# The first FFN product of three blocks by seven block products, with 40 listed V-moving heads

## The chip, the cores and the metric

One core of a Trainium2 chip runs the whole program. The core has a matmul engine (TensorE, in the profile PE, its weight loads PEld), a vector engine (VectorE, DVE), an activation engine (ScalarE, ACT), a third elementwise engine (GpSimd, POOL) and an engine whose queue issues most DMAs (SyncE, SP). The metric is the device time of one execution in microseconds (us), as a median of several runs. A difference of 0.2% is about what can be told from no difference here.

## What is computed

```python
xn = layernorm(x)                                   # x: 2048 x 512
q  = xn @ wq                                        # 32 heads of 128
p  = softmax(q @ k_cache^T / sqrt(128))             # 2048 cached keys a head
s  = concat_heads(p @ v_cache) @ wo                 # wo: 4096 x 512
h  = relu(xn @ w1 + b1) ** 2                        # w1: 512 x 1792
out = x + s * silu(h @ w2 + b2)                     # w2: 1792 x 512
```

Inputs and output are bf16. Attention and the feed-forward network (FFN) read the same normalized rows; the FFN's output gates the attention's.

## The kernel before

**Tiling.** The 2,048 query rows are four blocks j = 0 to 3 of 512 rows. A block runs the 32 heads in turn; head number g = 32 j + h goes from 0 to 127. A head's 2,048 keys are eight pairs of 128-key tiles, so the kernel has 1,024 *steps* (`NPAIR`), one for each pair. At a step `pi`, `gen_scores` (L903) issues two score matmuls of 512 columns into one half of `psA`, and one ACT exponential of 1,024 columns from there into one of 8 buffers `pT` (`NPT`). `gen_pv` (L1248) issues the product with V for the pair two steps earlier.

**Two kinds of heads.** In a *V-stationary* head (called b in the code, `gen_pv_b` L962) V is the weight and the exponentials move: 16 matmuls of 512 columns, with the result transposed in one bank of `psO`. ACT copies it to `o_col`. The softmax denominators then have to be summed apart: a pT buffer goes either to DVE alone (`den_part`, 1,024 columns) or through POOL, which adds its halves into `h_sum` (`part_add`), with a DVE reduction behind it (`part_half`). The sums travel through DRAM scratch (`d_scr`, `d_quad`, `r_scr`, `r_all`: four small DMAs) and POOL multiplies `o_col` by the reciprocals into `oT`. In a *V-moving* head (a) the exponentials are the weights and V with a column of ones moves: 64 matmuls of 129 columns, with the denominator in the 129th. DVE copies both `psO` banks to `o_un` (L1292), POOL scales, and one DMA transposes `o_bf` into `oT`. `at_a` (L499) chooses the kind while the order is being written: the first two and last three heads are V-moving, and others where the planner finds enough owed DVE work.

**The rest of TensorE's work** goes in between as *jobs* that use the two banks of `psF`: query projections, the FFN's first product (`job_h` L1434: 14 chunks of 128 hidden units, each four matmuls of 512 columns), its second (`job_o2` L1461) and the output projection (`job_wo` L1507). Jobs stand in a list with a due step and a release step (L1593-L1612); `fill_one` (L1620) takes matmuls from them at an even rate.

**The seven-product form.** In blocks 1 to 3 the query projection of two heads is done together (`job_pair` L1370): the 2x2 block product of weights (two heads by two halves of the 512 inputs) and rows (two halves of 256) takes seven block products instead of eight. Each block product is two matmuls of 256 columns, so 14 in all for a pair. For it, weights are scaled by a power of two from the heads' largest entry (`chunk_start` L829: DVE maxima, two trips through DRAM), ACT scales both heads (`wp_mul`), POOL makes four sums in f16 (`wp_sums`), and the whole goes to DRAM scratch `wq_scr` (`wp_store`), to be loaded a pair at a time (`fill_pair` L871). One staging area `wq_new` serves all 16 pairs, started every 22 steps from step 80. Sums of the rows are made by POOL once a block (`x_sums`). The results come out of `psF` through `u_t` by DVE copies and additions; `scaled` (L1364) gives a copy to ACT if ACT is planned to be free within `ACT_ROOM`.

**What sets the order.** The program writes each engine's queue beforehand. A planner (`_Sched` L111, costs in `_cost` and `_ISSUE`) keeps an estimated time for each engine and for each result, and `fill_dve`, `fill_pool`, `fill_sync` and `fill_act` (L1182-L1239) choose by these which waiting piece of side work is put into a queue next, within limits such as `ROOM`, `ACT_SPARE` and `SLACK`. On the chip the queues then run in the order written, each instruction waiting for its semaphores.

W1 is kept whole in `w1_sb`; its seven loads are issued between steps 0 and 48. `job_h` is evicted by two DVE instructions of 512 columns from `psF`: bias and relu into `r_t`, then (x + bias) times `r_t` into `h2T`.

## Time and profile before

| | us |
|---|---|
| median of 3 runs | 1216.28 (1214.98 to 1216.38) |
| the profiled execution | 1217.89 |
| its span, first to last instruction | 1216.0 |
| busy: TensorE / DVE / ACT / POOL | 1201.2 / 1074.1 / 1095.4 / 1044.5 |
| ACT: 1,024 columns of exponentials, one | 1.025 |
| DMA: mean busy share of the 16 engines, main queue | 84.8% |
| TensorE's granted clock | 1.000 |

| instruction (engine) | count | mean ns |
|---|---|---|
| h_sum from pT, 512 columns (POOL) | 636 | 1158 |
| d_part from h_sum, 512 columns (DVE) | 636 | 682 |
| d_part from pT, 1,024 columns (DVE) | 212 | 1212 |
| u_t from psF, 256 columns (DVE) | 144 | 457 |
| qt_sb from psF and u_t, 256 columns (DVE) | 144 | 453 |
| r_t from psF, 512 columns (DVE) | 56 | 726 |
| h2T from psF and r_t, 512 columns (DVE) | 56 | 746 |
| o_un from psO, 258 columns (DVE) | 44 | 420 |
| o_col from psO, 512 columns (ACT) | 106 | 595 |
| oT from o_col and r_all (POOL) | 106 | 1281 |
| weight scaling, 512 columns (ACT) | 32 | 718 |
| weight sums, 256 columns (POOL) | 64 | 670 |

The span is what one profiled execution took between its first and last instruction. An instruction is named by output and inputs, `psA<-qt_sb,kT` for a score matmul; L235 and L240 are the helpers that issue matmuls, so groups are told apart by their tiles. A busy share near 100% for TensorE is no sign of peak speed by itself, since the ends of matmuls overlap.

### The profile page before, as it was taken

The page shows a single profiled execution, that of the slowest core. Times are in us where ns is not written, and L with a number is a line of the kernel's source. Part 1 is how long each engine was busy: PE and PEld are TensorE (multiplying, and loading weights), DVE is VectorE, ACT ScalarE, POOL GpSimd, SP SyncE. Part 2 cuts the span into 40 slices and gives each one's busy share as a digit, 9 for nine tenths or more (in the row PEclk, how much of TensorE's full clock was granted, in tenths as well). Part 3 has the DMA queues.
Part 4 walks back from the last instruction along what each step waited for, and adds up shares of the span by engine and source line. Part 5 has one row for each costly group of instructions (what it writes and reads, how often), then busy time and mean ns, then how long its engine had stood idle before and what let it go on. Part 6 is the DMA issues. An engine that isn't in the chain of part 4 may idle for free.

```text
span 1216.0 us, 21110 instructions
## 1 busy us (share of the span) xinstructions
PE 1201.2 (99%) x6952; PEld 711.7 (59%) x7085; DVE 1074.1 (88%) x2019; ACT 1095.4 (90%) x1183; POOL 1044.5 (86%) x1008
## 2 busy tenths in 40 slices
PE   9999999999999999999999999999999999999999
PEld 7555555556666565665665555666556565655566
DVE  5999999998988979879899999877998989899973
ACT  7998999999999999999989989999998989899894
POOL 2889999999888979789879989877998989799973
PEclk9999999999999999999999999999999999999999
DMA  9799999889899989897888879887797987978871
GB/s 215 176 196 220 210 215 199 224 190 217 211 222 245 210 194 226 212 199 177 198 181 193 195 185 205 180 192 170 172 215 170 192 205 163 209 159 192 193 170 45
DMA packets 509020, 235.48 MB, mean 194 GB/s; under 512 B 399184, under 2 KB 485968, under 8 KB 508912
## 3 DMA queue, kind: packets, MB, share of 16 engines
q1 hardware_dynamic: 506816, 230.06, 84.8%
q0 software_dynamic: 1424, 3.81, 1.0%
q8 instruction: 56, 0.92, 0.3%
q14 instruction: 52, 0.43, 0.1%
q10 hardware_dynamic: 672, 0.26, 0.1%
HBM read 151.52 MB, written 11.46 MB: 134 GB/s over the span
## 4 chain that ended last, share of the span: by engine, by line
PE 94%; DVE 2%; DMA 2%; issue 1%; POOL 1%; SPq 0%; ACT 0%; ACTq 0%; DVEq 0%; POOLq 0%
PE psA L235 35%; PE psO L235 29%; PE psF L235 18%; PE psO L240 6%; PE psF L240 6%; DVE d_part L303 1%; DMA wq_sb<-in_A_wq_dram 1%; POOL h_sum L248 1%; DMA kT<-in_A_k_cache_dram 0%; SPq L311 0%; DMA wq_sb<-wq_scr 0%; PE psA L240 0%; ACT pT L244 0%; DVE qt_sb L258 0%; POOL acc L248 0%
## 5 line engine op out<-in xcount | busy, mean ns | idle before, releaser
L244 ACT ACTIVATE pT<-psA 128x1024 bf16<-128x1024 f32 x1025 | 1029.5, 1025 | 99.4 <-PE psA L235 69.4
L248 POOL TENSOR_TENSOR h_sum<-pT 128x512 f32<-128x512 bf16 x636 | 720.5, 1158 | 75.9 <-ACT pT L244 53.4
L235 PE MATMUL psA<-qt_sb,kT 128*128 128x512 bf16 x1963 | 591.6, 380 | 5.2 <-ACT pT L244 1.6
L235 PE MATMUL psO<-pT,v_sb 128*128 128x512 bf16 x1659 | 496.4, 379 | 2.6 <-DVE o_un L262 0.3
L303 DVE TRANSPOSE_TENSOR_REDUCE d_part<-h_sum 128x16 f32<-128x512 f32 x636 | 423.0, 682 | 12.8 <-POOL h_sum L248 12.3
L235 PEld LDWEIGHTS psA<-qt_sb,kT 128*128 128x128 bf16 x2032 | 277.2, 145 | 167.1 <-ACT pT L244 15.3
L303 DVE TRANSPOSE_TENSOR_REDUCE d_part<-pT 128x32 f32<-128x1024 bf16 x212 | 256.1, 1212 | 3.8 <-ACT pT L244 3.1
L235 PEld LDWEIGHTS psO<-pT,v_sb 128*128 128x128 bf16 x1696 | 165.6, 98 | 148.5 <-issue 2.3
L248 POOL TENSOR_TENSOR oT<-o_col,r_all 128x512 bf16<-128x512 f32 x106 | 135.7, 1281 | 32.4 <-DMA r_all<-r_scr 32.1
L235 PE MATMUL psF<-wo_all,oT 128*128 128x512 bf16 x468 | 154.7, 379 | 0.7
L240 PEld LDWEIGHTS psO<-v_sb,pT 128*128 128x128 bf16 x1408 | 93.9, 98 | 34.9 <-issue 0.4
L240 PE MATMUL psO<-v_sb,pT 128*128 128x129 bf16 x1408 | 108.2, 220 | 0.1
L235 PE MATMUL psF<-xnT,w_sb 128*128 128x512 bf16 x220 | 73.4, 379 | 0.2
L235 PE MATMUL psF<-w_sb,h2T 128*128 128x512 bf16 x215 | 70.9, 379 | 0.4
L253 DVE TENSOR_SCALAR u_t<-psF,sc_q 128x256 f32<-128x256 f32 x144 | 65.8, 457 | 5.8 <-PE psF L240 4.6
L235 PEld LDWEIGHTS psF<-wo_all,oT 128*128 128x128 bf16 x480 | 46.8, 98 | 40.6 <-DVE qt_sb L253 0.3
L240 PE MATMUL psF<-xs_t,wq_sb 128*128 128x256 f16 x384 | 69.7, 273 | 0.1
L258 DVE SCALAR_TENSOR_TENSOR qt_sb<-psF,sc_q,u_t 128x256 bf16<-128x256 f32 x144 | 65.2, 453 | 4.8 <-PE psF L240 3.6
L244 ACT ACTIVATE o_col<-psO 128x512 f32<-128x512 f32 x106 | 63.0, 595 | 0.0
L262 DVE COPY o_un<-psO 128x258 f32<-128x258 f32 x44 | 16.7, 420 | 50.1 <-PE psO L240 50.1
L240 PEld LDWEIGHTS psF<-xs_t,wq_sb 128*128 128x128 f16 (+1 forms) x384 | 36.8, 98 | 30.2 <-DVE u_t L253 3.6
L240 PE MATMUL psF<-xnT,wq_sb 128*128 128x256 bf16 x288 | 53.8, 273 | 0.4 <-DMA wq_sb<-wq_scr 0.4
(86 smaller groups left out, 753.6 us busy)
## 6 DMA issues: line engine op xcount, KB each, us to landing
v_sb<-in_A_v_cache_dram SPq DMA_DIRECT2D x508, 128.0 KB, 3.0
r_all<-r_scr SPq DMA_DIRECT2D x106, 256.0 KB, 4.0
wq_sb<-wq_scr SPq DMA_DIRECT2D x48, 448.0 KB, 4.3
wo_all<-in_A_wo_dram SPq DMA_DIRECT2D x64, 256.0 KB, 3.5
wq_scr<-wq_sb SPq DMA_DIRECT2D x16, 448.0 KB, 3.4
wq_sb<-in_A_wq_dram SPq DMA_DIRECT2D x16, 256.0 KB, 3.7
kT<-in_A_k_cache_dram SPq DMA_TRANSPOSE x254, 3.9
wq_sb<-in_A_wq_dram SPq DMA_DIRECT2D x31, 128.0 KB, 3.5
```

The costliest lines, as they stand in the source:

```text
L235: return e.matmul(out, lhsT, rhs, start=start, stop=stop)
L240: return e.matmul(out, lhsT, rhs, start=start, stop=stop, skip_group_check=True)
L244: return e.activation(out, in_, func, bias=bias, scale=scale)
L248: return e.tensor_tensor(out, in0, in1, op)
L253: return e.tensor_scalar(out, in0, scalar1=scalar1, scalar2=None, op0=op0)
L258: return e.scalar_tensor_tensor(out=out, in0=in0, scalar=scalar, in1=in1, op0=op0, op1=op1)
L262: return e.tensor_copy(out, in_)
L303: return e.tensor_reduce(out, in_, axis=AX.X, op=ALU.add, apply_transpose=True)
```

## The change

1. **FFN1 by pairs.** Block 0 keeps `job_h`. In blocks 1-3 a new `job_h2` computes two chunks of 128 hidden units by the seven-product form of `job_pair`. Its results are kept in fp32 in a new `hb_t` (bias added in the copies out of `psF`), and a DVE instruction `relu_sq` squares them into `h2T`. W1's columns are scaled by powers of two like the query weights: seven more pairs pass the staging, with maxima (`chunk_max`) over W1's chunks and over b1; b1 is scaled with them, and W2's rows are multiplied once by the inverse squares (`w2_mul`, ACT) after block 0's second product.
2. **W1 streamed.** `w1_sb` goes. W1 passes through two slots in the memory of `xs_t` during block 0; the scaled pairs are loaded one at a time into `w1_pair` (`fill_fpair`) in blocks 1-3.
3. **Staging.** Four staging areas instead of one, two of them borrowed until steps 190 and 215; 23 pairs, one every 13 steps from step 72.
4. **pT** has 10 buffers instead of 8. `r_t` shares memory with `hb_t`.
5. **o_col** is copied by DVE instead of ACT where the planner finds ACT later than DVE (plus `COL_ACT`).
6. **V-moving heads** are a written list of 40, ten in each block.
7. **Planner constants** and the planned issue time of `r_all` change. Every job has a list of what it waits for; `fill_one` takes a job only if all of it is planned ready by now (`SOON` = 0, was 100 ns), and `fill_act` may take any ready piece, W2's last.

```diff
-          "d_quad": (530, 4200), "r_scr": (530, 2200), "r_all": (1230, 4400)}
+          "d_quad": (530, 4200), "r_scr": (530, 2200), "r_all": (530, 4400)}
...
-    ROOM = 1500
+    ROOM = 1000
     LATE = 150
-    LATE_EVICT = 250
+    COL_ACT = -400
+    COL_DVE = 0
+    LATE_EVICT = 150
     POOL_ROOM = 300
-    SLACK = 1500
-    FIRST_B = 2
-    A_OWED = (14500, 12500, 12500, 14500)
-    LATE_U = 700
-    ACT_ROOM = 500
-    ACT_SPARE = 400
+    SLACK = 1000
+    A_SET = (0, 1, 8, 10, 12, 15, 17, 20, 26, 29, 33, 36, 38, 40, 42, 44, 46, 52, 60, 62, 66, 69, 71, 73, 75, 77, 81, 84, 90, 93, 97, 99, 102, 105, 107, 110, 119, 125, 126, 127)
+    LATE_U = 200
+    ACT_ROOM = 100
+    ACT_SPARE = 300
     PAIR_BANK = (0, 1, 0, 1, 0, 0, 1)
-    A_APART = 3
     NPP = H // 2
     NRW = 2 * HC
-    WQ_PACE = 22
-    WQ_FIRST = 80
+    WQ_PACE = 13
+    WQ_UNTIL = (9999, 190, 215, 9999)
+    SOON = 0
+    NO_ACT = (0,)
+    WQ_FIRST = 72
...
-    NSL, NSW, NQS, NPT, NOT, NOC, NHS = 3, 4, 5, 8, 21, 5, 3
+    NSL, NSW, NQS, NPT, NOT, NOC, NHS = 3, 4, 5, 10, 21, 5, 3
...
-    w1_sb = sb("w1_sb", [P, NDC, F], BF16)
...
+    w1_new = xs_t[:].rearrange("p i c q -> p (i c q)").bitcast(BF16).rearrange(
+        "p (s c e) -> p s c e", s=2, c=NDC)
+    w1_pair = sb("w1_pair", [P, PW], BF16)
+    wq_new2 = sb("wq_new2", [P, PW], BF16)
+    NFP = NFC // 2
+    hb_t = sb("hb_t", [P, 2, QB], F32)
...
-    r_t = sb("r_t", [P, 2, QB], BF16)
+    r_t = hb_t[:, 0, :].bitcast(BF16).rearrange("p (s q) -> p s q", s=2)
...
+        return g in A_SET
...
+    def chunk_max(c):
+        i, x = divmod(c, 2)
+        t_fm[c] = E(DV, partial(_abs_max, out=mx_f[:, c:c + 1],
+                                in_=w1_new[:, i % 2, :, x * P:(x + 1) * P]),
+                    deps=[tok_w1[i], t_max1])
...
+    def w2_mul(c):
+        t_w2s[c] = E(AC, partial(_act, out=w2_sb[:, c, :], in_=w2_sb[:, c, :], func=ACT.Copy,
+                                 scale=sc_2[:, c:c + 1]),
+                     deps=[t_o2[0, qt] for qt in range(TPB)] + [t_sc2[0], tok_w2])
+
+    def fill_fpair(j, i):
+        t_wf[j, i] = S.emit_dma(SP, partial(_dma, out=w1_pair[:], in_=wq_scr[NPP + i]), sl_wf,
+                                deps=[t_ws[NPP + i], t_fdone.get(fprev(j, i)), t_ws.get(wp_last.get(2))])
...
+            if max(AC.t - PE.t - COL_ACT, 0) > max(DV.t - PE.t - COL_DVE, 0):
+                t_free[b] = t_col[m] = E(
+                    DV, partial(_copy, out=o_col[:, m % NOC, :], in_=bankO(b)),
+                    deps=deps, late=LATE_EVICT)
+            else:
+                t_free[b] = t_col[m] = E(
+                    AC, partial(_act, out=o_col[:, m % NOC, :], in_=bankO(b), func=ACT.Copy),
+                    deps=deps)
...
+            for fn in sorted(act_quiet, key=lambda x: x.func is w2_mul):
+                t = ready_at(fn)
+                if t is not None and t <= max(AC.t, PE.t):
+                    act_quiet.remove(fn)
+                    fn()
+                    break
...
+    def relu_sq(j, c):
+        t_h2[j, c] = E(DV, partial(_stt, out=h2T[:, c, :], in0=hb_t[:, c % 2, :], scalar=0.0,
+                                   in1=hb_t[:, c % 2, :], op0=ALU.max, op1=ALU.mult),
+                       deps=[t_hc[j, c], t_hd[j, c]] + [t_o2[j - 1, qt] for qt in range(TPB)])
+
+    def biased(out, in_, c, deps):
+        if max(AC.t, S.ready(deps)) <= PE.t + ACT_ROOM:
+            return E(AC, partial(_act, out=out, in_=in_, func=ACT.Identity, bias=b1s[:, c:c + 1]),
+                     deps=deps)
+        return E(DV, partial(_ts, out=out, in0=in_, scalar1=b1s[:, c:c + 1], scalar2=None,
+                             op0=ALU.add), deps=deps, late=LATE_U)
+
+    def job_h2(j, i):
+        c = 2 * i
+        steps = pair_steps(w1_pair, j)
+
+        def mm(n, bank):
+            y, lhs, rhs, start = steps[n]
+            b = bank ^ y
+            place, place2 = bankF(b)[:, 0:HB], bankF(bank ^ 1)[:, 0:HB]
+            for k in range(2):
+                t = E(PE, partial(_mm_shared, out=place, lhsT=lhs[:, k, :], rhs=rhs(k),
+                                  start=start and k == 0, stop=k == 1),
+                      deps=[t_wf[j, i], t_xs[j], t_bankF[b]] + tok_xT[j], inc=k == 1)
+
+            def hb_of(x, q):
+                return hb_t[:, x, q * HB:(q + 1) * HB]
+
+            old = [t_hb[0]] if i == 0 and j == 1 else [
+                t_h2[fprev(j, i)[0], 2 * fprev(j, i)[1] + x] for x in range(2)]
+
+            def keep(x, ch):
+                t_us[x] = biased(u_t[:, x, :], place, ch, [t, t_us[x], t_b1s[0]])
+                return t_us[x]
+
+            def add(x, q, u):
+                t_us[u] = E(DV, partial(_tt, out=hb_of(x, q), in0=place2, in1=u_t[:, u, :],
+                                        op=ALU.add), deps=[t, t_us[u]] + old, late=LATE_U)
+                return t_us[u]
+
+            if n in (0, 2, 4):
+                t_bankF[b] = keep(n // 2, c + n // 4)
+            if n == 1:
+                t_bankF[b] = t_hn[0] = add(0, 0, 0)
+            if n == 4:
+                t_bankF[b ^ 1] = t_hn[1] = add(1, 1, 2)
+            if n == 5:
+                t_bankF[b] = t_x = biased(hb_of(1, 0), place, c + 1, [t, t_b1s[0]] + old)
+                t_hc[j, c + 1] = t_x
+                t_hd[j, c + 1] = t_hn[1]
+                calm(now[0] + 8, partial(relu_sq, j, c + 1))
+            if n == 6:
+                t_bankF[b] = t_hc[j, c] = add(0, 1, 1)
+                t_hd[j, c] = t_hn[0]
+                calm(now[0] + 8, partial(relu_sq, j, c))
+                t_fdone[j, i] = t_xuse[j] = t
+                n_xuse[j] += 1
+                nxt = (j, i + 1) if i + 1 < NFP else (j + 1, 0)
+                if nxt[0] < NQB:
+                    sync_quiet.append(partial(fill_fpair, *nxt))
...
-                  deps=[tok_w2, t_bankF[bank], t_h2[j, n]], inc=(n == NFC - 1))
+                  deps=[t_w2s[n] if j else tok_w2, t_bankF[bank], t_h2[j, n]], inc=(n == NFC - 1))
...
+    def h2_wait(j, i):
+        x = fprev(j, i)
+        return [t_wf.get((j, i)), t_xs.get(j), t_b1s[0]] + (
+            [t_h2.get((x[0], 2 * x[1] + y)) for y in range(2)] if x else [])
+
+    def o2_wait(j):
+        return [t_h2.get((j, c)) for c in range(NFC)] + (
+            [t_w2s.get(c) for c in range(NFC)] if j else [tok_w2])
...
-        for c in range(NFC):
+        for c in range(0, NFC, 1 if j == 0 else 2):
             k = b + (SPB * 9 // 256) * c
-            jobs.append((k, max(k - 130, 4), job_h(j, c), (None, j)))
+            job, w = (job_h(j, c), partial(h_wait, j, c)) if j == 0 else (
+                job_h2(j, c // 2), partial(h2_wait, j, c // 2))
+            jobs.append((k, max(k - 130, 4), job, None, w))
...
-        return S.ready(toks) <= PE.t + 100
+        return S.ready(toks) <= PE.t + SOON
...
+                if rel > step and not force:
                     continue
-                if rel <= step or force:
-                    cur[0] = [job, 0]
-                    cur_proj[0] = None if isinstance(p, tuple) else p
-                    jobs.pop(idx)
-                    break
+                toks = wait()
+                if None in toks or not soon(toks):
+                    continue
...
-    for i, k in enumerate([4, 10, 18, 28, 38, 48]):
-        at(k, partial(load_w1, i + 1))
+    at(4, partial(load_w1, 1))
+    for i in range(2, NFP):
+        at(30 + 18 * (i - 1) + 2, partial(sync_quiet.append, partial(load_w1, i)))
...
+    order = [0, 1, 2, 3]
+    for x in range(NFP):
+        order += [NPP + x, 4 + x]
+    order += range(4 + NFP, NPP)
+    last = {}
+    for x, p in enumerate(order):
+        k = WQ_FIRST + WQ_PACE * x
+        wp_stage[p] = [y for y in ((0, 3, 1, 2)[x % 4], x % 2 * 3) if k < WQ_UNTIL[y]][0]
+        if wp_stage[p] in last:
+            wp_prev[p] = last[wp_stage[p]]
+        last[wp_stage[p]] = p
+        at(k, partial(wp_start, p))
```

## The prediction

> **What bounds the kernel now.** I read the engines' busy times first, then the chain that ended last, then the starts in the timeline, and last the waits of the engine that the chain names.
>
> ```profile
> PE 1201.2 (99%) x6952; PEld 711.7 (59%) x7085; DVE 1074.1 (88%) x2019; ACT 1095.4 (90%) x1183; POOL 1044.5 (86%) x1008
> ...
> PE 94%; DVE 2%; DMA 2%; issue 1%; POOL 1%; SPq 0%; ACT 0%; ACTq 0%; DVEq 0%; POOLq 0%
> ```
>
> TensorE (PE) is busy for 99% and carries 94% of the chain. Matmuls overlap, so busy time does not say how much is slack. The start column does (TensorE's timeline, block 1):
>
> ```profile
> 315.15 0.62 PE L240 MATMUL psO<-v_sb,pT 128*128 128x129 bf16 x8
> 315.60 0.60 PE L235 MATMUL psA<-qt_sb,kT 128*128 128x512 bf16 x2
> 316.04 0.59 PE L235 MATMUL psF<-xnT,w_sb 128*128 128x512 bf16 x2
> 316.48 0.62 PE L240 MATMUL psO<-v_sb,pT 128*128 128x129 bf16 x8
> ...
> 322.64 0.60 PE L240 MATMUL psF<-xs_t,wq_sb 128*128 128x256 f16 x4
> 323.08 0.59 PE L235 MATMUL psO<-pT,v_sb 128*128 128x512 bf16 x2
> ```
>
> From start to start, two matmuls of 512 columns take 0.44 us, four of 256 take 0.44, eight of 129 take 0.45. Over the whole trace the start-to-start distances are 0.2158, 0.1093 and 0.0567 us for one of each. Counted by weight loads, of which none is missing: 4,792 of 512 columns (2,032 scores, 1,696 V-stationary PV, 496 output projection, 448 FFN, 120 query) make 1,034 us; 688 of 256, 75; 1,408 of 129, 80; the small ones about 12. Two more: some 2 ns on each score pair's first matmul, 2 us in all, and 2.5 us after the last matmul. That is 1,206 of 1,216. TensorE is the bound at matmul pace, and all its stalls together are some 10 us, 4 of them in the opening 15 us. The rest are small, with three larger ones. The waits and the timeline around one of them:
>
> ```profile
> PEld psA L235 <- ACT pT L244: 15.3, 49, 1.3
> ...
> PE psO L235 <- DVE o_un L262: 0.3, 1, 0.3
> ```
>
> ```profile
> 113.36 0.72 ACT L244 ACTIVATE wq_sb<-wq_sb,sc_q 128x512 bf16<-128x512 bf16 x1 [1.07 <-DMA wq_sb<-in_A_wq_dram]
> ...
> 113.99 1.00 ACT L244 ACTIVATE pT<-psA 128x1024 bf16<-128x1024 f32 x1
> ...
> 115.05 0.66 PE L235 MATMUL psA<-qt_sb,kT 128*128 128x512 bf16 x2 [0.80 <-ACT pT L244]
> ```
>
> ACT stood 1.07 us at a weight scaling whose load had not landed; the exponential behind it came late, and the scores behind that. The same happened at 218 us. Measured against the normal distance, TensorE lost 0.96 and 1.02 us there, and 0.60 at 318 us where the first pair's weights landed late.
>
> **TensorE's own work.** *FFN1 of blocks 1-3:* out go 3x14x4 = 168 matmuls of 512 columns, 168 x 0.2158 = 36.3 us. In come 21 pairs x 14 of 256 columns, 294 x 0.1093 = 32.1. Sum **-4.1**. All of it lies on the bound. *V-moving heads:* the trace has 22 (44 o_un copies), the list has 40. One costs 64 x 0.0567 = 3.63 us, a V-stationary one 16 x 0.2158 = 3.45; 18 x 0.173 = **+3.1**. Its two o_un evictions (420 ns each) hold up the next head's PV: the waits name 0.3 us in 22 heads, the start distances after such heads up to 0.9. For 18 more 0.2 to 0.9, I take **+0.4**, nearer the wait that is named, since the queue in front of these copies gets shorter.
>
> The Trainium skill, "TensorE: Matmul & The Clock Gate", section "Back-to-back issue gap", gives about 81 ns per matmul of 128 columns in a stream with weight loads, and about 131 for 512. By that an added head would cost 64 x 0.081 - 16 x 0.131 = 3.1 us, an estimate from that page, and 18 of them would lose some 56 us. The 56.7 and 215.8 ns of this trace, each with its own weight load, contradict both figures; the trace decides.
>
> **DVE.** Per V-stationary head: 6 halves at 682 and 2 whole tiles at 1212 ns (636 and 212 in 106 heads), sums, turn and reciprocal 1.06 us, together 7.6; per V-moving head 2 x 0.420 + 0.173 = 1.0. 18 heads save 118 us. FFN1 now costs 42 x (726 + 746) = 61.8 us there. After: per pair 4 biased copies (457, row of u_t), 3 additions (453, row of qt_sb from u_t) and 2 squarings of 512 fp32 from SBUF. The last has no row; the 512-column PSUM product at 746 is below, a scaling from SBUF that once took 1,786 ns beside GpSimd (xn_t: 401, median 437) is above. I take 1,000. 21 x (1.83 + 1.36 + 2.0) = 109. Column maxima: 14 x 650 ns = 9. Eviction of o_col moves here when the planner finds ACT late: 0 to 88 x 674 ns = 59. Net -118 + 47 + 9 + 0..59 = -62 to -3: DVE is at most as loaded as now, and most probably 30 us lighter.
>
> "SBUF — State Buffer", section "SBUF: two separate sides", says that a DVE instruction with two SBUF inputs and GpSimd's reads take one port pair in turn, the loser blocked for the whole instruction. The 1,786 ns above fits; by that rule each of 42 squarings could wait for a 1,158 ns h_sum, about 25 us of DVE in all if half do, an estimate, which the relief covers.
>
> **GpSimd (POOL).** A V-stationary head costs 6 x 1.158 + 1.281 = 8.2, a V-moving one 1.04 + 0.18 = 1.2; -126 us, and 28 weight sums at 670 ns add 19. It gets lighter by 107.
>
> **ACT.** Adds 14 W1 scalings and 14 W2 scalings, 28 x 718 = 20 us; 18 o_col fewer, -10.7; 0 to 88 x 595 ns go to DVE. "Either engine" for the biased copies will hardly happen: the same rule for the query pairs sent 192 of 192 to DVE, and the ACT limit in it is lowered.
>
> **SyncE and DMA.** 18 x 4 small DMAs of the denominators (about 0.43 us of issue each) go, 18 transposes (1.22) come: -31 + 22; 7 loads, 7 stores, 21 W1-pair loads (0.43) add 15. W1 streamed moves seven 256 KB loads later into block 0. Nothing here issues longer than now, and K and V are loaded two heads ahead.
>
> **Stalls.** Behind a pair's product stand TensorE's next scores and PV, so each bank wait costs directly. The query pairs lost 0.42, 0.29, 0.17, 0.17, 0.13 us in places where a u_t copy was late: 1.2 us in 48 pairs, so 21 more pairs 0.5; with the longer rule of bias and hb_t 0 to 1.5, **+0.7**. Out: with DVE lighter and ten pT buffers in place of eight these and the eight stalls of 0.09 behind ACT (1.9 together) should shrink, I take -1.5 (0 to -1.9). The three late loads (2.6): four staging places let a load run ahead, and ACT takes whichever scaling is ready; but there are 23 loads for 16 and the planner still counts on landing times. Half, -1.3 (+1.2, if two in 16 become three in 23, to -2.6). Together **-2.8**.
>
> Sum: -4.1 + 3.1 + 0.4 + 0.7 - 2.8 = -2.7 us. The profiled execution took 1,217.89 us (span 1,216.0 and 1.9 around it), so 1,215.2; the median of the runs is 1.6 below the profiled one: **1,213.6 us**. With every bound at its better end (-4.1 + 3.1 + 0.2 + 0 - 4.5) it is 1,211.0.
>
> **Rivals.** *(1) It comes out even.* Pair stalls at 1.5, evictions at 0.9, late loads not cured: -4.1 + 3.1 + 0.9 + 1.5 - 1.5 = -0.1, 1,216.2. For it: what the seven products save and the added heads cost nearly cancel by rows; against it: DVE and POOL lose 30 and 107 us of load. *(2) Slower: ACT becomes the bound between steps 72 and 358.* A step there lasts 1.17 us (32 heads of 8 steps from 17 to 309 us and to 608), an exponential 1.026: 0.142 x 286 = 41 us to spare. The scalings now come two in 13 steps for two in 22: 46 x 0.718 = 33, W2's 10, tanh 3, and 25 o_col at 0.595 = 15: 61. W2 can slip later (-10); if no o_col leaves ACT 10 us are missing, with half of them gone 3. TensorE has two score buffers, so it stands for what is missing: 1,216 to 1,224, I price it **1,220**. It decides where over a quarter of these o_col stay and the W2 scalings do not slip. For it: ACT is at 92-93% there now. Against: scalings are issued only when the planner finds ACT near TensorE. *(3) The gaps close nearly wholly:* 1,211.
>
> **Numbers.** Forecast, with its neighbours 1,212-1,213.8: 0.36. Rival 3: 0.09. Rival 1 (1,214-1,218.5): 0.27. Rival 2: 0.28, a third of it beyond 1,222. Some 0.2% (2.4 us) is what a measurement of this kernel tells from no change; so faster 0.45, same 0.27, slower 0.28. The range, 1,210.8 to 1,222, leaves out the far end of rival 2 and a little below. The likeliest case's own range is 1,211 to 1,215.
>
> **What would show it.** Right: 294 more matmuls of 256 columns at 0.109 us and 40 V-moving heads at 3.6; start-distance losses of TensorE after the opening under 5 us; DVE below 1,060, POOL near 940; h2T's squarings near 1 us; ACT's idle time still mostly ended by TensorE. Wrong: long waits of psA for pT between 90 and 430 us (rival 2), of psF for u_t or hb_t in blocks 1-3, or ACT standing for W1's staging loads (rival 1). The prediction fails if the planner's order, made for other durations, makes a queue stand that no row of now shows.

## The result, and the profile after

The changed kernel takes 1249.4 us (median; 1248.96 to 1252.04) against 1216.33: a ratio of 1.0278, interval 1.026 to 1.0296. Forecast were 1213.6, range 1,210.8 to 1,222. The span of the profiled execution is 1247.2 us, 31.2 more than before.

Page of the kernel after, busy times and the chain that ended last:

```profile
PE 1217.3 (98%) x8075; PEld 756.5 (61%) x8075; DVE 1063.3 (85%) x2071; ACT 1073.6 (86%) x1107; POOL 1015.5 (81%) x1003
...
PE 78%; DMA 9%; DVE 6%; POOL 3%; SPq 2%; issue 1%; ACT 1%; POOLq 0%; ACTq 0%; DVEq 0%
```

Every engine's share fell, and TensorE carries 78% of the chain where it carried 94%; DMA went from 2 to 9%. So no engine has taken TensorE's place: TensorE waits, and what it waits for begins with transfers. Its matmuls are as fast as before (0.2158, 0.1093 and 0.0567 us from start to start).

**Where the time went.** Counting every start-to-start distance that is over 0.5 us too long, TensorE lost 3.9 us in 5 stalls before and 27.2 in 19 after. The granted clock fell too: it was half from 22.7 to 29.5 us and from 169.4 to 172.9 us, and 1.00 elsewhere until the last 2 us. TensorE stood until 24.1 and 169.8 us, so it worked 8.4 us at half the clock and lost 4.2 us by it. 23.3 us more of stalls, these 4.2 and the -1.0 of its own work (-4.1 + 3.1) make 26.5 of the 31.2 us; the rest is not assigned. By the start of a head's scores, after minus before: +6.3 us at head 2, +0.9 at head 12, +18.3 at head 32, +27.2 at head 64, +31.3 at head 124. The dip is only work put off: by 121 us, 32 of FFN1's 56 matmuls of block 0 had run, 56 before (24 x 0.2158 = 5.2 us). Nearly all is lost in blocks 0 and 1.

The first stall. VectorE's timeline of after, then TensorE's:

```profile
22.93 0.69 DVE L299 TENSOR_REDUCE mx_f<-xs_t 128x1 f32<-128x512 bf16 x1 [2.35 <-DMA xs_t<-in_B_w_dram]
23.53 0.75 DVE L262 COPY o_un<-psO 128x258 f32<-128x258 f32 x2
```

```profile
18.53 0.62 PE L240 MATMUL psO<-v_sb,pT 128*128 128x129 bf16 x8
...
24.09 1.02 PE L240 MATMUL psO<-v_sb,pT 128*128 128x129 bf16 x8 [4.29 <-DVE o_un L262]
```

The new column maximum of W1 stands at the head of DVE's queue and waits for its load; the copies that free `psO` stand behind it. After the stall eight matmuls take 1.02 us instead of 0.62: the clock went with it. The longest stall after 120 us, 2.8 us at 167 us, is of the same kind: a column maximum waits 3.8 us for a later load of W1, and the `o_un` copies behind it come late.

A typical later one, SyncE's (SP) timeline of after and TensorE's:

```profile
137.77 0.43 SPq L312 DMA_DIRECT2D wq_sb<-in_A_wq_dram  x1
138.25 1.94 SPq L316 DMA_TRANSPOSE kT<-in_A_k_cache_dram  x1
140.23 0.58 SPq L312 DMA_DIRECT2D d_scr<-d_row  x1
140.85 0.93 SPq L312 DMA_DIRECT2D v_sb<-in_A_v_cache_dram  x1
141.82 1.59 SPq L312 DMA_DIRECT2D xs_t<-in_B_w_dram  x1
```

```profile
141.08 0.65 PE L235 MATMUL psA<-qt_sb,kT 128*128 128x512 bf16 x2
143.93 0.61 PE L235 MATMUL psF<-xnT,wq_sb 128*128 128x512 bf16 x2 [2.20 <-DMA wq_sb<-in_A_wq_dram]
```

TensorE needed at 141.7 a weight load that SyncE issued at 137.77 and that landed 6.1 us later. Look at the second column of the first fence: one issue follows the other with 0.05 us between. Summing the spaces of over 70 ns between the end of one issue and the start of the next, SyncE had 0.0, 0.4 and 1.0 us free in 76-137, 137-198 and 198-259 us (before: 0.8, 2.3, 3.6). In those 183 us it spent 170.9 us in issues and 10.5 in the small spaces, over 18.1 heads (counted by score matmuls): **10.0 us a head**, where TensorE needs about 9.5 (183 us for the 19.25 heads of before) and SyncE had used 9.2 before. (The expectations of e13 and e14 have 10.1 and 9.3, from slightly smaller counts of heads.) In a queue that is never free, issue time per head and elapsed time per head are the same number, so this says that SyncE is full, not yet why.

Two readings of the issues help. The number a head did not grow: 13.5 in that stretch in both kernels. At the mean lengths of before, the mix of after would take only some 0.2 us a head more (an estimate: its counts times the means of before); the other 0.6 us is issues that took longer, the K transposes 1.55 us in the mean for 1.39. And this is not SyncE standing for a K buffer: a buffer is free when a head's scores have ended, and each of the transposes with a semaphore wait that took over 1.5 us began at least 1.5 us after the last such end. What made the issues longer stays open.

The waits of after, whole span:

```profile
PEld psA L235 <- ACT pT L244: 17.8, 32, 2.7
...
DVE mx_f L299 <- DMA xs_t<-in_B_w_dram: 9.1, 5, 3.8
...
PEld psF L235 <- DMA wq_sb<-in_A_wq_dram: 5.8, 4, 2.6
...
ACT wq_new L244 <- DMA wq_new<-in_A_wq_dram: 4.9, 2, 3.0
```

The first row is hardly longer than before (15.3) but its longest wait is 2.7 us for 1.3: such a wait begins with a weight scaling on ACT, last row, that waits for its load in front of the exponential.

### The profile page after: what moved, and what is told of

It is laid out like the page before. It is cut to its first block, busy times and chain, and to the rows that moved or that the text cites. A ratio compares the mean times of both kernels' runs of the same rounds, so it can differ in the third digit from the quotient of the medians.

```text
span 1247.2 us, 22940 instructions
## 1 busy us (share of the span) xinstructions
PE 1217.3 (98%) x8075; PEld 756.5 (61%) x8075; DVE 1063.3 (85%) x2071; ACT 1073.6 (86%) x1107; POOL 1015.5 (81%) x1003
## 4 chain that ended last, share of the span: by engine, by line
PE 78%; DMA 9%; DVE 6%; POOL 3%; SPq 2%; issue 1%; ACT 1%; POOLq 0%; ACTq 0%; DVEq 0%
PE psA L235 29%; PE psO L235 21%; PE psF L235 12%; PE psO L240 8%; PE psF L240 7%; DVE d_part L304 2%; DMA d_quad<-d_scr 2%; POOL h_sum L248 1%; DMA d_scr<-d_row 1%; SPq L312 1%; DMA xs_t<-in_B_w_dram 1%; DMA wq_sb<-in_A_wq_dram 1%; ACT pT L244 1%; DMA r_all<-r_scr 1%; DMA r_scr<-d_rec 1%
## 5 line engine op out<-in xcount | busy, mean ns | idle before, releaser
L244 ACT ACTIVATE pT<-psA 128x1024 bf16<-128x1024 f32 x1025 | 1031.2, 1022 | 144.3 <-PE psA L235 107.0
L248 POOL TENSOR_TENSOR h_sum<-pT 128x512 f32<-128x512 bf16 x584 | 673.0, 1172 | 116.9 <-DVE d_part L304 59.2
L235 PE MATMUL psO<-pT,v_sb 128*128 128x512 bf16 x1408 | 419.6, 380 | 5.3 <-DVE o_un L262 5.2
L304 DVE TRANSPOSE_TENSOR_REDUCE d_part<-h_sum 128x16 f32<-128x512 f32 x584 | 388.9, 684 | 7.0 <-POOL h_sum L248 6.9
L235 PEld LDWEIGHTS psO<-pT,v_sb 128*128 128x128 bf16 x1408 | 137.4, 98 | 122.6 <-issue 10.8
L240 PE MATMUL psO<-v_sb,pT 128*128 128x129 bf16 x2560 | 198.2, 221 | 4.5 <-DVE o_un L262 4.3
L240 PEld LDWEIGHTS psO<-v_sb,pT 128*128 128x128 bf16 x2560 | 171.9, 98 | 50.6 <-issue 6.3
L304 DVE TRANSPOSE_TENSOR_REDUCE d_part<-pT 128x32 f32<-128x1024 bf16 x120 | 143.9, 1208 | 3.2 <-ACT pT L244 2.9
L248 POOL TENSOR_TENSOR oT<-o_col,r_all 128x512 bf16<-128x512 f32 x88 | 112.5, 1279 | 34.6 <-DMA r_all<-r_scr 31.9
L258 DVE SCALAR_TENSOR_TENSOR qt_sb<-psF,sc_q,u_t 128x256 bf16<-128x256 f32 x144 | 68.7, 477 | 10.5 <-PE psF L240 6.9
L262 DVE COPY o_col<-psO 128x512 f32<-128x512 f32 x86 | 59.0, 687 | 20.1 <-PE psO L235 19.1
L248 POOL TENSOR_TENSOR o_bf<-o_un,rden 128x512 bf16<-128x512 f32 x37 | 39.0, 1054 | 17.0 <-DVE rden L266 16.9
```

The source lines that it names most:

```text
L235: return e.matmul(out, lhsT, rhs, start=start, stop=stop)
L240: return e.matmul(out, lhsT, rhs, start=start, stop=stop, skip_group_check=True)
L244: return e.activation(out, in_, func, bias=bias, scale=scale)
L248: return e.tensor_tensor(out, in0, in1, op)
L258: return e.scalar_tensor_tensor(out=out, in0=in0, scalar=scalar, in1=in1, op0=op0, op1=op1)
L262: return e.tensor_copy(out, in_)
```

## The experiments

All results together. "Free" is SyncE's free time in 76-137, 137-198 and 198-259 us, in per cent; stalls are TensorE's over 0.5 us, summed by the time at which they begin, for 0-40, 40-120, 120-320, 320-500 us and later. Ratios are to the kernel before, timed beside each run.

| run | us | ratio (interval) | SyncE free % | stalls us |
|---|---|---|---|---|
| before | 1216.3 | | 1 / 4 / 6 | 3.9: 1.3, 1.0, 1.6, 0, 0 |
| after | 1249.4 | 1.0278 (1.026-1.0296) | 0 / 1 / 2 | 27.2: 4.5, 3.1, 13.4, 4.6, 1.6 |
| e1 | 1265.1 | 1.0386 (1.0361-1.0412) | 0 / 1 / 0 | 38.4: 4.3, 2.8, 13.0, 10.9, 7.5 |
| e2 | 1225.3 | 1.0069 (1.0046-1.0093) | 3 / 5 / 10 | 6.6: 0, 1.7, 1.5, 2.8, 0.6 |
| e3 | 1231.1 | 1.0121 (1.0093-1.0149) | 0 / 5 / 7 | 8.8: 0.6, 0, 3.3, 4.9, 0 |
| e4 | 1267.4 | 1.0398 (1.0361-1.0436) | 0 / 8 / 9 | 38.1: 0, 4.5, 16.7, 11.9, 5.0 |
| e5 | 1221.4 | 1.0031 (1.0016-1.0046) | 0 / 1 / 2 | 5.7: 0, 0.8, 4.9, 0, 0 |
| e6 | 1231.6 | 1.0105 (1.0076-1.0134) | 1 / 1 / 6 | 9.3: 0.5, 1.1, 5.7, 2.0, 0 |
| e7 | 1220.9 | 1.0022 (1.0012-1.0031) | 0 / 2 / 2 | 2.9: 0.6, 1.7, 0, 0, 0.6 |
| e8 | 1250.8 | 1.0271 (1.0249-1.0293) | 0 / 1 / 4 | 28.5: 0, 4.4, 16.5, 6.9, 0.7 |
| e9 | 1256.0 | 1.0314 (1.0296-1.0332) | 0 / 1 / 2 | 34.3: 4.2, 5.0, 16.6, 6.3, 2.1 |
| e10 | 1220.8 | 1.0034 (1.0023-1.0046) | 0 / 1 / 1 | 3.3: 0, 0, 3.3, 0, 0 |
| e11 | 1256.6 | 1.0331 (1.0307-1.0355) | 0 / 1 / 0 | 34.4: 0, 5.1, 13.6, 11.8, 4.0 |
| e12 | 1243.3 | 1.0213 (1.0196-1.023) | 0 / 1 / 0 | 23.9: 0, 2.7, 12.6, 3.3, 5.4 |
| e13 | 1247.1 | 1.0242 (1.0224-1.0261) | 5 / 7 / 12 | 27.3: 4.7, 7.3, 1.7, 11.1, 2.5 |
| e14 | 1222.9 | 1.0045 (1.0029-1.0061) | 11 / 22 / 15 | 7.2: 0.6, 1.6, 1.8, 3.2, 0 |
| e15 | 1236.4 | 1.015 (1.0128-1.0172) | 1 / 9 / 12 | 20.7: 5.2, 2.8, 5.0, 4.3, 3.4 |
| e16 | 1229.3 | 1.0094 (1.0076-1.0112) | 3 / 9 / 13 | 15.7: 0.7, 2.5, 5.6, 5.1, 1.9 |
| e17 | 1237.7 | 1.0167 (1.0151-1.0183) | 1 / 2 / 7 | 16.4: 0.5, 0.6, 7.4, 4.2, 3.7 |
| e18 | 1233.1 | 1.0134 (1.0118-1.015) | 6 / 15 / 24 | 10.4: 0.5, 2.6, 1.4, 5.9, 0 |

**First theory: the planned issue of `r_all`.** SyncE's order is too tight because 0.7 us of reserve per V-stationary head went.

e1, the kernel after:
```diff
-          "d_quad": (530, 4200), "r_scr": (530, 2200), "r_all": (530, 4400)}
+          "d_quad": (530, 4200), "r_scr": (530, 2200), "r_all": (1230, 4400)}
```


> The changed kernel, with only the planned issue time of r_all set back from 530 to 1230 ns; the work is the same, the order differs. Theory (SyncE's queue is full between 76 and 260 us, and the order supposes that its DMAs are issued 2 to 3 us sooner than they are): the order now leaves SyncE 0.7 us more for each of 88 loads, and the stalls of TensorE behind late loads shrink by half or more: 1225 to 1236 us. Rival A (the 16 DMA engines are full, whatever the queue): 1246 to 1252. Rival B (DVE stands at the new column maxima until W1 lands, above all at 19 us): the stall of 4.3 us stays, 1243 to 1250. Rival C (18 more V-moving heads cost it): 1246 to 1252.

1265.1 us, worse by 16. The theory as stated falls.

e2, the kernel before:
```diff
-          "d_quad": (530, 4200), "r_scr": (530, 2200), "r_all": (1230, 4400)}
+          "d_quad": (530, 4200), "r_scr": (530, 2200), "r_all": (600, 4400)}
```


> The kernel before, with only the planned issue time of r_all cut from 1230 to 600 ns; the work is the same. Theory (the high value was the room that covered SyncE's other, underrated issues): slower than before by 3 to 12 us, 1219 to 1228, with new waits for loads in block 0. Rivals A, B and C, none of which lies in the order: 1215 to 1218.

1225.3, as the theory said. But an edit that costs 8 us in one kernel and whose reverse costs 16 in the other has no price of its own: each moves the whole written order, and other loads come late.

**The 40 heads alone.** e3, the kernel before:
```diff
     def at_a(g):
-        if g not in a_set:
...
-        return a_set[g]
+        return g in A_SET
```


> The kernel before, with only its choice of heads replaced by the written list of 40 V-moving heads. Theory (SyncE): its 18 transposes at 1.2 us take the place of 72 small DMAs at 0.43, so SyncE has a little less to do; TensorE pays 3.1 us of pitch: 1216 to 1222. Rival C (the heads cost it, by evictions and the order around them): 1228 to 1248. Rivals A and B: 1216 to 1222, as the theory.

1231.1: by the ratio 14.7 us, 3.1 of them matmul pitch. Timeline of e3, SyncE, ACT and TensorE at its largest stall:

```profile
396.13 1.99 SPq L311 DMA_DIRECT2D wq_sb<-in_A_wq_dram  x1
...
402.70 0.72 ACT L244 ACTIVATE wq_sb<-wq_sb,sc_q 128x512 bf16<-128x512 bf16 x1 [4.45 <-DMA wq_sb<-in_A_wq_dram]
...
404.38 1.07 PE L235 MATMUL psA<-qt_sb,kT 128*128 128x512 bf16 x2 [4.09 <-ACT pT L244]
```

A staging load lands 6.5 us after its issue began; ACT's scaling, written ahead of the exponentials, waits 4.45 us, and TensorE 4.09; half clock for 3.4 us follows. It is the mechanism of 113 us in the kernel before, four times as long. This one event is worth some 6 of the 14.7 us.

**Fewer issues on SyncE?** e4, the kernel after, three staging calls (W1 loads, `wp_load`, `wp_store`):
```diff
-            SP, partial(_dma, ...
+            GP, partial(_dma, ...
```


> The changed kernel, with the loads of W1 and of the 23 pairs to be scaled and the 23 stores to wq_scr issued by GpSimd's queue in place of SyncE's (53 DMAs, some 25 us of SyncE's issue in the first 420 us, 31 us of GpSimd's). Theory (SyncE's queue): the backlog in block 0 goes, and 12 to 24 us come back: 1225 to 1238. Rival A (DMA engines full): the transfers are the same, 1245 to 1252. Rival B (DVE at the maxima): W1's loads leave a little sooner, 1240 to 1248. Rival C: 1246 to 1252.

1267.4. SyncE had 75 and 68 issues for 83 and 79 in 76-198 us, yet no time free until 137 us: its K transposes now took 1.82 and 1.89 us there (1.53 and 1.63 in after). The first stall was gone, the time lost after it. The Trainium skill, "DMA: Bandwidth & Descriptors", section "Issuing engines are not separate DMA queues", says that a second issuing engine saves only the sequencer's own time, usually small beside the transfer. e4 agrees in so far as nothing more was gained; it did not even save SyncE's time, which stayed at 9.4 us of issues a head. "Small" holds for one transfer here too (a V load takes 0.5 us to issue and 3.3 us to land in after), but the issues of a head add up to what TensorE needs for a head. The run also puts these transfers into the queue of the engine that makes the softmax sums, so it changes more than SyncE.

**Issues or bytes, in the kernel before.** e5 and e6 (the code shortened):
```diff
+    def dm_store(x):
+        S.emit_dma(SP, partial(_dma, out=dm_scr[x, 0:R, 0:C], in_=B_w1[0:R, 0:C]), sl_dm)
+    for x in range(12):
+        at(72 + 16 * x, partial(dm_store, x))   # e5: R, C = 1, 2; e6: 128, 1792
```


> The kernel before with 12 more transfers on SyncE's queue, one every 16 steps from step 72 (about 85 to 240 us), each of 4 bytes from device memory to device memory; nothing waits for them, they cost the planner nothing, and every other instruction keeps its place in its queue. Theory (in blocks 0 and 1 the 16 DMA engines are full, and SyncE is late because its issues are held back by them): some 12 x 0.5 us of issue more on a queue that had 1.4 to 5.9% of its time free in that stretch, 1216 to 1220 us. Rival (SyncE's queue is late by the number of its issues, whatever they move): 1220 to 1228 us, and no more than 2 us less than with 12 large transfers.

> The same 12 transfers on SyncE's queue in the same places, but of 448 KB each, the size of a staging store, some 1.3 us of all 16 DMA engines apiece, 15.6 us together. It moves bytes and computes nothing. Theory (full DMA engines): 1222 to 1234 us, at least 4 us more than with the 12 small ones. Rival (number of issues): within 2 us of the run with the small ones. Third case (neither binds): both 1216 to 1218 us.

1221.4 and 1231.6: by the ratios +3.8 and +12.8 us. Twelve issues cost nearly 4 us, their bytes 9 more: e5 lies in the rival's range, e6 in the theory's. (The profiled execution of e6 took 1226.5 us, 5 less than the median.) Windows of e5, then of e6 (last columns: granted clock, busy share of the DMA engines, GB/s):

```profile
137.00:198.00 61.00, 59.28 (x276) 31.24 (x275) 59.17 (x100) 55.55 (x63) 57.39 (x57) 1.00 0.91 204
```

```profile
137.00:198.00 61.00, 58.62 (x270) 30.38 (x268) 57.70 (x100) 54.33 (x61) 56.43 (x56) 1.00 1.01 229
```

So this kernel had no room in that stretch for either, and I took full DMA engines for the cause.

**Heads elsewhere.** e7, the kernel before with the list used for `g >= 64` only.


> The kernel before, with the listed V-moving heads only in blocks 2 and 3 (9 more than it has there: 20 for 11), its own rule in blocks 0 and 1. Theory (a head more costs its matmul pitch, 0.173 us, and its output transpose hurts only where the DMA engines are full, in blocks 0 and 1; in blocks 2 and 3 they were busy 0.82 to 0.90): 1216.3 + 9 x 0.17 = 1217.9, so 1216 to 1220 us. Rival (a V-moving head costs some 0.8 us wherever it stands, as 15 us for 18 would have it): 1222 to 1226 us.

+2.7 us by the ratio, 0.3 a head (0.17 by pitch): a little above the theory, far below the rival. By subtraction the other 9 heads of e3, in blocks 0 and 1, stand for the other 12, half of it the one stall at 400 us; the two orders differ in more than these heads.

**The first stall alone.** e8, the kernel after:
```diff
         for c in (2 * i, 2 * i + 1):
-            calm(now[0] + 16, partial(chunk_max, c))
+            if i < 2:
+                at(now[0] + 8, partial(calm, now[0] + 24, partial(chunk_max, c)))
+            else:
+                calm(now[0] + 16, partial(chunk_max, c))
```


> The kernel after, with VectorE's column maxima of the first two loads of W1 queued 8 steps later, behind the copies of o_un that they stood in front of. Theory (the wait of 4.3 us at 19 us, with the colder clock behind it, some 3.7 us, adds to the end): 1241 to 1243 us against 1249.4. Rival (the time is given back at the next late load, since the queue of SyncE only gets tighter when TensorE is earlier): 1247 to 1251 us.

1250.8: no gain. Head 2 starts 7.0 us earlier than in after, head 32 only 1.4. Something that paces blocks 0 and 1 takes the time back.

**Fewer bytes, as many issues.** e9 (after) and e10 (before):
```diff
-                SP, partial(_dma, out=dst[:, x * n:(x + 1) * n, :],
+                SP, partial(_dma, out=dst[0:P // 2 if 9 <= g < 48 else P, x * n:(x + 1) * n, :],
...
```


> The kernel after, with the loads of V of heads 9 to 47 moving only the first 64 of 128 partitions (four loads a head, 64 KB each instead of 128); the other half of V keeps an earlier head's numbers. Every instruction keeps its place; about 256 KB a head less for the 16 DMA engines, some 1.5 us of their 9.5 us a head by the packet times, from 95 to 450 us. Theory (the DMA engines' load in blocks 0 and 1 holds SyncE's issues back and makes the late loads): 1218 to 1230 us against 1249.4. Rival (the written order itself, whatever the load: an engine's queue in the wrong order, or the number of SyncE's issues): 1242 to 1250 us.

> The same halved loads of V for heads 9 to 47 in the kernel before, as a control: its TensorE lost some 4 us to late loads after the opening, so 1212 to 1217 us by the theory, a gain of at most a fifth of that of the kernel after. Rival (half loads make any kernel of this kind faster by the same): a gain as large as there.

1256.0 and 1220.8: both slower, and outside every range given. Windows of after, then of e9:

```profile
76.00:137.00 61.00, 56.95 (x401) 34.24 (x399) 51.73 (x105) 51.13 (x54) 43.90 (x46) 1.00 0.98 215
137.00:198.00 61.00, 55.63 (x341) 30.98 (x340) 45.86 (x90) 49.46 (x55) 44.97 (x52) 0.97 0.99 219
```

```profile
76.00:137.00 61.00, 53.40 (x369) 32.05 (x375) 50.30 (x100) 48.87 (x51) 42.07 (x45) 1.00 0.86 182
137.00:198.00 61.00, 53.67 (x338) 30.49 (x342) 44.29 (x88) 46.31 (x50) 43.04 (x48) 0.97 0.87 191
```

The DMA engines are down to 0.86 (0.98 in after) and TensorE stalls as much. So full DMA engines alone are not the bound of the kernel after. But SyncE was not relieved either: the K transposes took it 1.40 us for 1.55, a V load of half the bytes 0.62 for 0.51, and its issues of a head rose from 9.4 to 9.8 us.

**A planner that knows.** e11: `"kT": (1500, 3900)` for `(1230, 3400)` in the kernel after. e12: the same with `WQ_PACE = 15` and e8's edit.


> The kernel after, with the planner told that a transpose of K holds SyncE for 1.50 us and lands 3.9 us after its start (1.23 and 3.4 in the kernel): what the trace of after shows in 76 to 259 us. Nothing that is computed changes; only the order written by hand is laid out anew. Theory in the form that the order is wrong because the planner underrates SyncE: 1228 to 1240 us. Theory in the form that the traffic itself is too much there, however ordered: 1242 to 1256 us.

> The kernel after, with the planner's cost of the K transposes as in the run before (1.50 and 3.9 us), the staging one pair every 15 steps instead of 13, and the column maxima of the first two loads of W1 queued 8 steps later. Theory (spread traffic, and an order that knows of it): 1224 to 1238 us, below the run with the cost alone. Rival (neither helps, as the same bytes come later): 1242 to 1256 us.

1256.6 and 1243.3. Telling the planner gives nothing; slower staging and the later maxima together 13 us against e11, still with SyncE full, above the expected range and in the rival's.

**Half the V issues, the same bytes.** e13 (after), e14 (before), e15 (e13 with `"kT": (1400, 3900)`):
```diff
-    NKP, NVP, NWP = 2, 4, 4
+    NKP, NVP, NWP = 2, 2, 4
...
-        if part == 2 and at_a(g):
+        if part == 1 and at_a(g):
```


> The kernel after, with the V of a head loaded in 2 transfers of 256 KB instead of 4 of 128 KB: the same bytes, and all is computed as before. New theory (SyncE's issuing is the bound in block 0): from 76 to 259 us SyncE spent 170.9 us in issues and 10.5 us in the small gaps between them over 17.9 heads, 10.1 us a head, where TensorE needs some 9.5; two issues less a head save 2 x (0.50 + 0.045) = 1.1 us, which leaves 9.0. Then 1220 to 1234 us against 1249.4. Rivals (the DMA engines' bytes, or the written order of the other engines): 1243 to 1256 us.

> The same 2 loads of V a head in the kernel before, as a control. Its SyncE spent (166.4 + 10.4) / 18.9 = 9.3 us a head in that stretch, just under what TensorE needs, and TensorE lost some 4 us to late loads: 1213 to 1220 us by the new theory, since the planner's own end moves by +2.8 us with it. By the rivals the same: this run is the measure of what the edit does where SyncE does not bind.

> The kernel after with 2 loads of V a head and the planner told that a transpose of K holds SyncE for 1.40 us (1.23 in the kernel), which lays the order out anew; its own planned end is 4.2 us earlier than with the 2 loads alone. New theory: 1216 to 1232 us, and no worse than the run with the loads alone by more than 4 us. Rivals: 1243 to 1256 us.

This is the run that tells. In e13 SyncE has 5 to 12% free, at a DMA share of 1.03 to 1.07 in 76-259 us, more than in after:

```profile
76.00:137.00 61.00, 53.74 (x350) 31.64 (x356) 49.30 (x98) 46.76 (x51) 44.38 (x46) 0.97 1.05 221
137.00:198.00 61.00, 60.19 (x390) 36.16 (x397) 49.68 (x104) 54.80 (x58) 47.44 (x54) 1.00 1.07 222
```

TensorE's stalls of 40-320 us go from 16.5 to 9.0 us. (The column of 120-320 us alone, 13.4 to 1.7, says too much: a stall of 3.0 us begins at 118.5 us in e13.) Of the 9.0, 6.1 are two waits for streamed loads of W1. Between the starts of heads 2 and 32, after loses 12.0 us against before and e13 4.2. In e14 the same edit gains nothing in that stretch (stalls of 2.6 and 3.4 us).

Each run has another written order, so this could be one lucky order. Set side by side, it is not: between these two heads the seven versions of the kernel after with four V loads a head (after, e1, e4, e8, e9, e11, e12) lose 9.9 to 18.5 us against before, the four with two (e13, e15, e16, e17) 1.9 to 4.3. So the number of transfers that SyncE has to issue is worth some 8 us there, and their bytes are not. Two cautions. A cost of each transfer, whichever engine issues it, would do the same: e4 left SyncE as few issues in 76-259 us (212, as e13; 244 in after) and lost 18.5. And little free time is no measure of a loss by itself: e7 and e10 had 0 to 2% free and lost 0 and 2.5 us there.

The total hardly moved (1247.1, outside the theory's range and inside the rivals'), because new stalls came at 320-500 us, 11.1 for 4.6. e14 missed its range too (1222.9 for 1213 to 1220). Timeline of e13 at the largest of the new stalls, SyncE, ACT, DVE, TensorE:

```profile
438.26 0.43 SPq L312 DMA_DIRECT2D wq_new<-in_A_wq_dram  x1
...
444.66 0.72 ACT L244 ACTIVATE wq_new<-wq_new,sc_q 128x512 bf16<-128x512 bf16 x1 [3.64 <-DMA wq_new<-in_A_wq_dram]
...
446.46 0.39 DVE L248 TENSOR_TENSOR hb_t<-psF,u_t 128x256 f32<-128x256 f32 x1
...
446.90 0.61 PE L240 MATMUL psF<-xs_t,w_pair 128*128 128x256 f16 x2 [4.57 <-DVE hb_t L248]
```

Again a scaling stands in ACT's queue for a late staging load; exponentials, the sums on POOL and DVE, and the addition that frees `psF` come late one after the other. That is the order, not SyncE's load: e15's order has 4.3 us there, and 1236.4 (its range: 1216 to 1232).

**The first stall again, now with SyncE relieved.** e16: e15 with e8's edit.


> The kernel of the run with 2 loads of V a head and 1.40 us for a K transpose (1236.4 us), with the column maxima of the first two loads of W1 queued 8 steps later. In the kernel after, whose SyncE had no time free, that edit gave nothing. Theory (with time free on SyncE the first stall, 3.9 us there, and the colder clock behind it now come off the end): 1229 to 1233 us. Rival (the time is given back again at the waits for W1's stream near 100 to 160 us): 1235 to 1239 us.

1229.3, 7.1 less, as the theory said; in e8 the same edit gave nothing. So the stall counted where SyncE was relieved behind it, and not where it was full. What is left in e16: three waits for streamed loads of W1, 7.1 us together, the longest 4.35 us (SyncE's and TensorE's timeline),

```profile
153.24 0.43 SPq L312 DMA_DIRECT2D xs_t<-in_B_w_dram  x1
...
157.56 0.61 PE L235 MATMUL psF<-xnT,xs_t 128*128 128x512 bf16 x1 [4.35 <-DMA xs_t<-in_B_w_dram]
```

issued just as TensorE reached it (W1 was resident before), and 5.1 us at 320-500.

e17: e16 with `(1500, 4600)` for K, `(520, 4200)` for V and 5,000 ns for transfers without a row.


> The kernel after with 2 loads of V a head, the first maxima later, and a planner that reckons with 1.50 us of issue and 4.6 us to land for a K transpose, 4.2 us for a load of V, and 5.0 us (4.0) for every transfer that has no row of its own, W1's and the staging's among them. Its own planned end is 1214.1, 6 us later than that of the run before. Theory (what is left of the loss is loads that land later than the order assumes): 1220 to 1230 us, within 15 us of its planned end. Rival (the bytes or SyncE): 1235 to 1250 us.

1237.7: missed, and in the rival's range. SyncE is nearly full again until 198 us in this order (1 / 2 / 7% free), and longer landing times in the plan do not help. Yet its stalls of 40-320 us, 8.0, are no more than e16's 8.1; it loses more behind that (head 64 starts 14.6 us later than in before, in e16 8.7).

e18: e3 with e13's edit.


> The kernel before with the 40 listed V-moving heads and 2 loads of V a head. With 4 loads the 40 heads cost 14 us (1231.1 against 1217); with 2 loads and its own heads the kernel took 1222.9. Theory (the heads cost 3.1 us of matmul pitch, and the rest is SyncE's issue time for their output transposes): 1225 to 1231 us. Rival (the bytes of the transposes, or the order around the heads): 1235 to 1239 us.

1233.1, between the two expectations: 10.2 us above e14, where e3 stood 14.7 above the kernel before. By the medians at most a third of the heads' cost is SyncE's issue time, and with 3.4 us either way on e3 hardly that is clear; 5.9 us of stalls at 320-500 stay. What these come from in that kernel is left open.

No version here beats the kernel before.

## Why the prediction was wrong

- **The step that failed:** "Nothing here issues longer than now, and K and V are loaded two heads ahead", in the part on SyncE and DMA. I added up counts (-31 + 22 + 15 us of issue over the whole span) and never set them against the room in the stretch where the change puts them. SyncE was 94 to 99% taken in 76-259 us already, at 9.2 us a head where TensorE needs 9.5. By counts the change adds some 0.2 us a head there, which would still have fitted. What the sentence had wrong is the length of an issue: the K transposes took 1.55 us for 1.39, and issues that take longer are 0.6 us a head, so SyncE passed TensorE's pace (10.0 us a head) and the loads came late, two heads ahead or not. Two V loads a head instead of four take 8 us of the loss away (e13; e15 to e17 lose as little there); e9 shows that lower traffic alone does not. Why the issues became longer stays open.
- **Late loads, taken at -1.3 (+1.2 to -2.6):** the right mechanism with the wrong sign and size. Stalls over 0.5 us, most of them behind late loads, rose by 23.3 us. The sentence under "what would show it", that the planner's order could make a queue stand, was the case that came; I gave it no price and no chance.
- **V-moving heads, +3.1 and +0.4:** the pitch was right, the price was not: e3 measured 14.7 us. e7 puts 0.3 us a head in blocks 2 and 3, so by subtraction the rest hangs on blocks 0 and 1, some 6 us of it on one late staging load. I had costed their transposes as issues, not what a changed order pushes back.
- **The wait of DVE's new maxima** was counted as busy time only (9 us, relieved). It stood in front of the `psO` copies: 4.3 us, and the clock behind it, 7.1 us together once it counts (e16).
- **Rival 2** had the direction, not the mechanism: ACT is not the bound (86% busy; its idle time is ended mostly by TensorE's scores, 107.0 of 144.3 us). Eviction moved 86 of 88 `o_col` to DVE.
- **Right:** FFN1's 294 matmuls at 0.109 us and 40 heads; squarings at 1.15 us for 1.0 (0.64 to 0.68 us each where no GpSimd instruction ran beside them, up to 2.65 where one did; 21 us in all above the short ones, where the prediction had 25); DVE 1063, just above the 1,060 I had named. POOL fell to 1015, not 940.

Of the 33 us, this is shown: about 8 before head 32 by the number of V loads (stalls of 40-320 us 16.5 to 9.0), read here as SyncE's issue time, and 7 by the first stall where SyncE is relieved. e15's order, with the same work as e13's, is 11 us faster, and no single cause is shown for that. e16 keeps 11.4 us (1.0094); its trace shows 7.1 us of waits for W1's stream and 5.1 us of stalls at 320-500 us, where before had 3.9 us of stalls in all, and neither was taken out singly. The terms do not add up alone: e1, e2 and e17 show that each new order brings stalls of its own.

## What to carry to other kernels

Before adding transfers to an issuing queue, sum its issues in the stretch where they come, per head or per step, and set that beside the matmuls of the same stretch; a queue that is 95% taken there has no cheap issue left (twelve of 4 bytes cost 3.8 us in e5). Take the issue lengths from the loaded stretch, and expect them to move. A stall removed ahead of a stretch that the queue paces can be worth nothing until the queue is relieved (e8, e16). And an instruction that waits for a load at the head of an in-order queue costs what is queued behind it, not its own length.

## What the hardware showed beyond that

**The clock drops after short stalls.** TensorE's timeline of e18, after a gap of 2.39 us:

```profile
114.39 0.66 PE L235 MATMUL psA<-qt_sb,kT 128*128 128x512 bf16 x2 [2.39 <-ACT pT L244]
...
115.58 1.06 PE L235 MATMUL psA<-qt_sb,kT 128*128 128x512 bf16 x2
116.44 1.06 PE L235 MATMUL psF<-xnT,wq_sb 128*128 128x512 bf16 x2
117.29 1.06 PE L235 MATMUL psO<-pT,v_sb 128*128 128x512 bf16 x2
118.14 0.77 PE L235 MATMUL psA<-qt_sb,kT 128*128 128x512 bf16 x2
118.75 0.59 PE L235 MATMUL psF<-xnT,wq_sb 128*128 128x512 bf16 x2
```

Pairs start 0.86 us apart instead of 0.43 until 118.4. The granted clock was 0.50 from 115.07 to 118.49 us, so a stall of 2.4 us costs 1.7 us more. The gap of 2.76 us at 167 us of after did the same (granted clock 0.79 in 166-172 us, 0.93 in 172-178), that of 2.20 us at 141 us did not (1.00).

The length of the gap alone does not decide. In all 20 traces the half clock lasts 3.41 us or twice that, apart from the last few us of a span, so time can be cut into pieces of 3.41 us, counted from where the clock changed. The stall of after at 141 us lies in two pieces, 0.6 us in one and 1.8 in the next. One of e17, shorter by starts (2.16 us at 254.4 us for 2.36), lies in one piece, 253.6 to 257.0 us, and the clock was 0.50 from there to 260.4. Over all traces, behind their first 8 us, a piece at full clock was followed by half the clock where TensorE stood 2.16 us of it or more (35 pieces), and by full clock where it stood 2.14 us or less. The Trainium skill, "TensorE: Matmul & The Clock Gate", section "What's actually happening", has the clock halved after an idle window of about 3.4 us; the pieces have that length, but 2.2 us of idle in one were enough, and the measurement decides.

**An issue has no fixed length.** The mean K transpose took SyncE 1.39 us before, 1.55 after and 1.8 to 1.9 with GpSimd issuing beside it (e4), with the same operands in 76-259 us. A V load over 64 partitions was no faster to issue than one over 128: 0.62 us for 0.51 in e9 against after, 0.55 for 0.52 in e10 against before. In both runs other plain issues became longer too (the weight loads' mean 0.56 us in e10 for 0.45), so the shape is not shown to be the reason.
